# A parameters' stage rearranged: casts and a reciprocal moved between engines, unit 0's table parts sent within SBUF, and a stream loaded later

## The chip, the cores and the metric

The kernel runs on one core of one Trainium2 chip. The metric is the device time of the whole program in microseconds (us), as the median of several runs. Beside the runs there is one profiled execution, in which the hardware profiler records every instruction with its engine, its start and its duration. Engines are named as in the profile: PE (TensorE), DVE (VectorE), ACT (ScalarE), POOL (GpSimd), and SP (SyncE), which only issues DMAs here. "Line L283" is line 283 of the kernel before.

## The reference, cut to what matters

A stream x of 2048 positions by 640 channels passes through four layers: a state-space convolution, a multi-query attention, and both again with the same weights. Each layer normalises its input and adds its result to the stream. What the change touches is the kernel K of the convolution:

```
dt = exp(log_dt)[:, None]                  # 640 channels
logdA = dt * (A_re + 1j * A_im)            # 640 x 128 states
dB = dt * (B_re + 1j * B_im)
P = exp(logdA[:, :, None] * l)             # l = 0 .. 2047
K = einsum("dn,dnl,dn->dl", C, P, dB).real
```

So K[d, l] is a sum over 128 states of |C B dt| exp(dt A_re l) cos(dt A_im l + angle of C B). The rest of a convolution layer is a transform of K and of x, a product, and the transform back, plus x times Dskip.

## The kernel before, in words

**Stages.** `kgen` makes K for all 640 channels and takes about the first 268 us. After it come the first convolution with the spectra of K, an attention layer, the second convolution and the second attention. The change lies in `kgen`, in two places.

**The parameters' stage** (`kg_tables`, L254 to L361). Its tiles are 128 partitions by 640 values: 5 groups of 128 channels, 128 states in each row. It computes five quantities per channel and state: `thr`, the phase step in turns without its whole part; `th1`, the step of 32 positions; `ph`, a phase at the start which contains the angle of C B; `are`, the decay per position; and `lw`, the logarithm of the size of C B dt. The angle comes from an arctangent of the smaller over the larger of |re| and |im|, for which L310 takes a reciprocal on DVE. Each quantity is then split into three BF16 parts whose sum is the float32 value: `cast` writes part k into `hs[n][:, k]` on ACT, `rest` subtracts it on DVE, and so on for three parts. In the kernel before the casts of `ph` and `lw` are `tensor_copy` on DVE.

**The tables.** A unit of work needs the parts with channels in the partitions' place: `tb` (48 rows: three parts of `th1` for 16 channels), `ta` (96 rows: `thr`, then `ph` from row 48) and `tm` (96 rows: `are`, then `lw`). Each is indexed by q, eight groups of 16 partitions of the parameters' tiles. Unit u reads group q = u mod 8. `send` brings `th1`, `thr` and `are` there through DRAM: one DMA writes the whole of `hs[n]` to a DRAM tile `hd...`, and three read it back, one for each part, into all eight q. `send_late` brings `ph` and `lw` straight from SBUF to SBUF, three DMAs of 20 KB for each q. The order on SP in the kernel before: `th1` by DRAM, `thr` by DRAM, the write of `are`, `ph` for q = 0, the three reads of `are`, `lw` for q = 0, and then `ph` and `lw` in turn for q = 1 to 7.

**The units** (`_kgen`, from L394). There are 20 units of 32 channels. For each, PE multiplies the table parts by constants `kg` into PSUM: phases (`phase_first`, L422, one PSUM tile for both halves h) and sizes (`sizes`, L461). DVE turns a phase into an integer fraction of a turn (`turns`, L431, and `fraction`, L436, into tiles `f`), ACT takes sines (`trig`, L446 and L447), squares (L454) and exponentials (`exps`, L469 and L471), DVE multiplies (`products`, L490 to L494), and PE sums over the states (`sums`, L504). `store` (L513) is ACT's copy of a finished unit from PSUM into `kst`; units 0 to 3 share the first `kst`, and `store(0)` stands ahead of all other ACT work in the turn u = 3 of the loop. Sines and exponentials need different activation tables on ACT; each switch is an ACT_TABLE_LOAD. A loop written out by hand (`manual_schedule`) fixes the order of PE, ACT and DVE in the units' loop, and that of ACT, DVE and SP in `kg_tables`. Instructions of the other engines are ordered by the framework, and it is free to place a DMA of SP between those of `kg_tables` where no hand-written order covers it.

**The stream.** `load_x` (L711 to L716) reads x in eight DMAs, two for each group g of four tiles. It is called in the turn u = 0, outside SP's written order, and the framework put its DMAs among those of the parameters' stage: four at the start, one after the write of `th1`, one after that of `thr`, one after `ph` for q = 0, and one after the last `lw`. `stats(t)` are DVE's statistics of tile t of x for the first normalisation: six in the turn u = 0, four in the turn after the last unit, the other six during the first convolution.

**Buffers.** The parameters' tiles live in a pool `kgq` that is closed when `kg_tables` is done; the units' pool `bp` is opened after that and takes the same place in SBUF. The pool's option `reuse_waits="tile"` makes the first writer of each buffer wait for the last users of what lay there. In `kgq` the tiles of `hs` come first, in the order ph, lw, th1, thr, are. In `bp` the two buffers of `kst` come first (8 KB for each partition), then in the kernel before the four of `f` (4 KB each).

Of the kernel before, what the change touches and what calls it, by code (L numbers as in the profile page):

```python
# [21 lines left out]
P = 128  # L22
L = 2048
D = 640
NST = 128
# [177 lines left out]
class Net:  # L203
# [47 lines left out]
        with ExitStack() as ctx:  # L251
            self._kgen(ctx)

    def kg_tables(self, pp, hs, t3, SH, ldt, aim, are_raw, bre, bim, cre, cim, ta, tb, tm):  # L254
# [9 lines left out]
        ar, ai, mx, mn, gt = (t3(n) for n in ("ar", "ai", "mx", "mn", "gt"))  # L264
        res = {n: t3("res" + n) for n in hs}

        def cast(n, src, k):
            A(hs[n][:, k], src if k == 0 else res[n], AF.Copy)

        def rest(n, src, k):  # L270
            V(res[n], src if k == 0 else res[n], hs[n][:, k], ALU.subtract)

        def send(n, dst, between=lambda: None):
            hd = self.dr.tile([P, 3, 5 * NST], BF16, name="hd" + n)
            nc.sync.dma_start(hd, hs[n].rearrange("p k t s -> p k (t s)"))
            between()
            for k in range(3):
                nc.sync.dma_start(dst[16 * k : 16 * k + 16].rearrange("d q t s -> d q (t s)"),
                                  hd[:, k].rearrange("(q d) x -> d q x", d=16))

        def send_late(q, dst, h):
            for k in range(3):
                nc.sync.dma_start(dst[48 + 16 * k : 64 + 16 * k, q].rearrange("d t s -> d (t s)"),  # L283
                                  h[16 * q : 16 * q + 16, k].rearrange("d t s -> d (t s)"))

        A(dt, ldt, AF.Exp)
        for t in range(5):
            T(th[:, t], aim[:, t], dt[:, t : t + 1], 1.0 / TWO_PI, ALU.mult, ALU.mult)
        V(wr, cre, bre, ALU.mult)
        self.frac(pp, thr, th, SH)  # L290
        T(th1, thr, 32.0, None, ALU.mult)
        self.frac(pp, th1, th1, SH)
        cast("th1", th1, 0)
        V(u0, cim, bim, ALU.mult)
        V(wr, wr, u0, ALU.subtract)
        A(ar, wr, AF.Abs)
        V(wi, cre, bim, ALU.mult)
        V(u0, cim, bre, ALU.mult)
        V(wi, wi, u0, ALU.add)
        A(ai, wi, AF.Abs)  # L300
        rest("th1", th1, 0)
        cast("th1", th1, 1)
        V(mx, ar, ai, ALU.max)
        V(mn, ar, ai, ALU.min)
        T(mx, mx, 1e-37, None, ALU.max)
        rest("th1", th1, 1)
        cast("th1", th1, 2)
        send("th1", tb)
        cast("thr", thr, 0)
        nc.vector.reciprocal(u0, mx)  # L310
        V(u0, mn, u0, ALU.mult)
        for t in range(5):
            A(are[:, t], are_raw[:, t], AF.Copy, scale=dt[:, t : t + 1])
        cast("are", are, 0)

        A(u1, u0, AF.Arctan)
        V(gt, ai, ar, ALU.is_gt)
        rest("thr", thr, 0)
        cast("thr", thr, 1)
        T(wr, wr, 0.0, 0.5, ALU.is_lt, ALU.mult)  # L320
        S(u1, gt, 0.5 * math.pi, u1, op0=ALU.mult, op1=ALU.subtract)
        A(u1, u1, AF.Abs, scale=1.0 / TWO_PI)
        T(wi, wi, 0.0, -2.0, ALU.is_lt, ALU.mult)
        rest("thr", thr, 1)
        V(u1, wr, u1, ALU.subtract)
        A(u1, u1, AF.Abs)
        cast("thr", thr, 2)
        send("thr", ta)
        T(ph, th1, 32.0, None, ALU.mult)
        self.frac(pp, ph, ph, SH)  # L330
        S(u1, wi, 1.0, u1, op0=ALU.add, op1=ALU.mult)
        V(ph, ph, u1, ALU.add)
        self.frac(pp, ph, ph, SH)

        A(u2, u0, AF.Square)
        A(lw, mx, AF.Ln)
        A(u3, u2, AF.Ln, bias=1.0)
        nc.vector.tensor_copy(hs["ph"][:, 0], ph)
        rest("ph", ph, 0)
        nc.vector.tensor_copy(hs["ph"][:, 1], res["ph"])  # L340
        rest("ph", ph, 1)
        nc.vector.tensor_copy(hs["ph"][:, 2], res["ph"])
        rest("are", are, 0)
        cast("are", are, 1)
        S(lw, u3, 0.5, lw, op0=ALU.mult, op1=ALU.add)
        for t in range(5):
            T(lw[:, t], lw[:, t], ldt[:, t : t + 1], None, ALU.add)
        rest("are", are, 1)
        cast("are", are, 2)
        send("are", tm, lambda: send_late(0, ta, hs["ph"]))  # L350
        nc.vector.tensor_copy(hs["lw"][:, 0], lw)
        rest("lw", lw, 0)
        nc.vector.tensor_copy(hs["lw"][:, 1], res["lw"])
        rest("lw", lw, 1)
        nc.vector.tensor_copy(hs["lw"][:, 2], res["lw"])
        for q in range(8):
            if q > 0:
                send_late(q, ta, hs["ph"])
            send_late(q, tm, hs["lw"])

    def _kgen(self, ctx):  # L361
        tc, nc, ins = self.tc, self.nc, self.ins
# [8 lines left out]
        kg = sp.tile([96, 2560], BF16, name="kg")  # L371

        with tc.tile_pool(name="kgq", bufs=1) as pp:
            SH = [P, 5, NST]
# [16 lines left out]
            with tc.manual_schedule(engines={mybir.EngineType.Activation, mybir.EngineType.DVE,  # L391
                                             mybir.EngineType.SP}):
                self.kg_tables(pp, hs, t3, SH, ldt, raw["A_A_im"], raw["A_A_re"], bre, bim, cre, cim,
                               ta, tb, tm)  # L394

        bp = ctx.enter_context(tc.tile_pool(name="kgb", bufs=2, reuse_waits="tile"))


        units = [(q, r, q * 256 + 16 * r, 128, 128) for q in range(2) for r in range(8)]
        units += [(2, r, 512 + 16 * r, 64, 64) for r in range(4)]  # L400
        C1, S1, C2, S2, M1, M2, E1R, F, PH, PE_, PK, KST = ({} for _ in range(12))
        KST[0, 0] = bp.tile([P, 64, 32], F32, tag="kst", bufs=2, name="kst00")

        def big(tag, u, x, bufs=2):
# [4 lines left out]

        def fl(a):  # L410
            return a.rearrange("p d a s -> p (d a) s")

        def grp(table, u, par, rows):
            d = units[u][2] + par * units[u][3]
            return table[0:rows, d % 128 // 16, d // 128]

        def phase_first(u, h):

            pp = PH[u, h] = kp.tile([P, 1024], F32, tag="ph", bufs=1, name=f"ph{u}{h}")
            src, col, rows = ((tb, 0, 48), (ta, 512, 96))[h]  # L420
            for par in range(2):
                nc.tensor.matmul(pp[:, 512 * par : 512 * par + 512], grp(src, u, par, rows),  # L422
                                 kg[0:rows, col : col + 512], start=True, stop=True)

        def turns(u, h):

            if (u, h) not in PH:
                phase_first(u, h)
            pp = PH.pop((u, h))
            f = F[u, h] = bp.tile([P, 1024], I32, tag="f", bufs=4, name=f"f{u}{h}")  # L430
            nc.vector.tensor_scalar(f, pp, 2.0**23, None, ALU.mult)  # L431

        def fraction(u, h):

            f = F[u, h]
            nc.vector.tensor_scalar(f, f, 9, 9, ALU.logical_shift_left, ALU.arith_shift_right)  # L436

        def trig(u, h):
            if h == 0:
# [88 lines left out]
        n = len(units)  # L528
        engines = {mybir.EngineType.PE, mybir.EngineType.Activation, mybir.EngineType.DVE}
        with tc.manual_schedule(engines=engines):  # L530
            for h in range(2):
                turns(0, h)
                fraction(0, h)
            left = []

            def fill():
# [3 lines left out]
            for u in range(n + 3):  # L540
                now, nxt, prod, tot = u < n, u + 1 < n, 0 < u <= n, 2 <= u < n + 2
                odd = u % 2 == 1
                if u == 0:
                    self.load_x()
# [163 lines left out]

        return dram.rearrange("(i h t) d -> h i t d", h=2, t=16)

    def load_x(self):  # L711
        nc = self.nc
        for g in range(4):
            for jh in range(2):
                nc.sync.dma_start(self.x[64 * jh : 64 * jh + 64, 4 * g : 4 * g + 4],
                                  self.rows(self.ins["A_u"])[jh][:, 4 * g : 4 * g + 4])  # L716
# [968 lines left out]
```

## Time and profile before

| | us |
|---|---|
| median of 3 runs | 2933.86 |
| lowest and highest | 2932.78, 2934.31 |
| the profiled execution's own time | 2934.5 |
| its span, first to last instruction | 2932.7 |
| busy in the span: PE, ACT, DVE | 2690.0, 2378.7, 2350.0 |
| ACT's first sine (L446) | starts at 46.34 |
| ACT's first write of kst (L513) | starts at 80.34 |
| last write of kst | starts at 268.53 |

How to read the views. The page gives the span and the busy time of each engine. The windows cut the span into stretches: the busy time of each engine with the number of its instructions, the granted clock, the share of the DMA engines that was busy, and GB/s. The timeline lists instructions in order of time: start, duration, engine, line, operation, out<-in by the program's names, and in brackets the idle time of the engine before it with what ended that. An engine's name with a q behind it (SPq, ACTq) stands for its sequencer, which issues DMAs and waits; that is not counted as busy. The waits group idle times: who waited for whom, us in total, times, the longest. For SPq these are the times that the queue of DMA issues stood still. The view of a line gives durations in ns as smallest, median and largest, then the first and last start in us.

### The profile page before, as it was taken

The numbers are of one execution on the slowest core, as the hardware profiler recorded it, in microseconds if no ns is written. First come the engines' busy times: TensorE is split into PE (matmuls) and PEld (weight loads), VectorE is DVE, ScalarE is ACT, GpSimd is POOL, SyncE is SP. The second block draws the span as 40 slices with busy tenths as digits, with TensorE's granted clock in tenths as the row PEclk, the third lists the DMA queues.
The fourth block names the chain that finished last, engine by engine and source line by source line (L and its number), as shares of the span: only waits on it lengthen the run. The fifth ranks groups of instructions, "written<-read, shape, count | busy, mean of one in ns | idle before, by whom it ended". The sixth has DMA issues, their size and how long they took to land. (4 is left out here: it accounts for less than half of the span.)

```text
span 2932.7 us, 71549 instructions
## 1 busy us (share of the span) xinstructions
PE 2690.0 (92%) x29916; PEld 1561.1 (53%) x29916; DVE 2350.0 (80%) x2819; ACT 2378.7 (81%) x2905; POOL 293.9 (10%) x514
## 2 busy tenths in 40 slices
PE   2667989998899999999999998998999999999999
PEld 0335979774344444444444787764444444444444
DVE  8998999935688888878888699726888888888885
ACT  5996432546899999999999624338999999999997
POOL 0000011000111110101011101001101111111111
PEclk9668999998999999999999999998999999999999
DMA  6115544442211111111111346231111111111211
GB/s 148 36 31 159 216 101 108 129 135 71 88 34 34 38 34 34 35 35 33 37 32 31 100 108 164 68 128 47 32 37 38 49 34 35 52 35 36 55 30 32
DMA packets 156101, 196.31 MB, mean 67 GB/s; under 512 B 66220, under 2 KB 123532, under 8 KB 152148
## 3 DMA queue, kind: packets, MB, share of 16 engines
q1 hardware_dynamic: 119704, 141.90, 16.1%
q0 software_dynamic: 33776, 48.08, 7.6%
q8 instruction: 239, 3.92, 0.5%
q10 hardware_dynamic: 2288, 1.64, 0.2%
q14 instruction: 94, 0.77, 0.1%
HBM read 111.47 MB, written 48.55 MB: 55 GB/s over the span
## 5 line engine op out<-in xcount | busy, mean ns | idle before, releaser
L1390 ACT ACTIVATE ring<-ring 128x1024 f32<-128x1024 f32 (+1 forms) x680 | 739.8, 1088 | 0.4 <-DVE ring L1381 0.3
L1365 ACT ACTIVATE pt<-scb 128x1024 f32<-128x1024 f32 x684 | 693.3, 1115 | 25.6 <-PE scb L1355 23.6
L1365 ACT ACTIVATE pt<-scd 128x1024 f32<-128x1024 f32 x684 | 699.9, 1135 | 13.6 <-PE scd L1355 11.8
L1381 DVE COPY ring<-scd 128x1024 f32<-128x1024 f32 x307 | 375.4, 1223 | 81.9 <-PE scd L1355 56.4
L1381 DVE COPY ring<-scb 128x1024 f32<-128x1024 f32 x307 | 374.9, 1221 | 79.8 <-PE scb L1355 59.6
L1355 PE MATMUL scb<-qpb,kt 62*128 62x512 f32 x2048 | 365.3, 445 | 28.8 <-DVE ring L1381 14.1
L1355 PE MATMUL scd<-qpd,kt 62*128 62x512 f32 x2048 | 364.3, 444 | 18.1 <-ACT pt L1365 6.8
L1421 PE MATMUL pob<-pt,vt 128*32 128x256 f32 x5472 | 368.0, 387 | 0.0
L1421 PE MATMUL pod<-pt,vt 128*32 128x256 f32 x5472 | 367.4, 386 | 0.0
L1355 PEld LDWEIGHTS scb<-qpb,kt 62*128 62x128 f32 x2048 | 169.9, 186 | 248.0 <-ACT pt L1365 133.0
L1355 PEld LDWEIGHTS scd<-qpd,kt 62*128 62x128 f32 x2048 | 169.3, 186 | 238.8 <-ACT pt L1365 142.2
L1407 DVE SCALAR_TENSOR_TENSOR zh<-zh,zm 128x1024 f32<-128x1024 f32 x198 | 239.9, 1211 | 0.0
L1421 PEld LDWEIGHTS pob<-pt,vt 128*32 128x32 f32 x5472 | 143.3, 109 | 168.4 <-issue 109.7
L1421 PEld LDWEIGHTS pod<-pt,vt 128*32 128x32 f32 x5472 | 143.2, 109 | 165.9 <-issue 107.1
L1421 PE MATMUL pob<-ring,vt 128*32 128x256 f32 x2456 | 164.8, 381 | 0.4 <-ACT ring L1390 0.4
L1421 PE MATMUL pod<-ring,vt 128*32 128x256 f32 x2456 | 163.9, 379 | 0.4 <-ACT ring L1390 0.4
L1453 POOL DMA_DIRECT2D dn<-on x62 | 43.6, 703 | 1189.0 <-DVE on L1452 1151.8
L1459 POOL DMA_DIRECT2D rc<-ivd x248 | 126.4, 516 | 113.4 <-DMA ivd<-dn 109.4
L1490 DVE TENSOR_TENSOR x<-pyd,x 128x320 f32<-128x320 f32 x147 | 71.8, 488 | 77.2 <-PE pyd L1503 77.1
L1490 DVE TENSOR_TENSOR x<-pyb,x 128x320 f32<-128x320 f32 x147 | 71.8, 489 | 76.5 <-PE pyb L1503 76.4
L1503 PE MATMUL pyb<-wo,ot 128*32 128x320 f32 x1176 | 106.7, 434 | 6.1 <-DVE on L1452 5.5
L1503 PE MATMUL pyd<-wo,ot 128*32 128x320 f32 x1176 | 106.7, 434 | 5.4 <-DVE on L1452 4.6
(388 smaller groups left out, 4086.1 us busy)
## 6 DMA issues: line engine op xcount, KB each, us to landing
Akh<-kh SPq DMA_DIRECT2D x10, 2048.0 KB
rc<-ivd POOLq DMA_DIRECT2D x248, 64.0 KB, 2.2
kh<-Ak SPq DMA_DIRECT2D x5, 2048.0 KB
qhd<-qh SPq DMA_DIRECT2D x40, 256.0 KB
qld<-ql SPq DMA_DIRECT2D x40, 256.0 KB
qpb<-qhd SPq DMA_DIRECT2D x256, 40.0 KB
qpd<-qhd SPq DMA_DIRECT2D x256, 40.0 KB
ot<-on SPq DMA_DIRECT2D x216, 40.0 KB
```

What stands on the lines that cost most here:

```text
L1355: nc.tensor.matmul(sc[:, 512 * par : 512 * par + 512], kt[rows, 128 * t : 128 * t + 128], qps[nb, hg][rows, f].rearrange("p a c -> p (a c) ...
L1365: nc.scalar.activation(pt, sc, AF.Exp, scale=SCALE)
L1381: nc.vector.tensor_copy(cols, sc)
L1390: nc.scalar.activation(cols, cols, AF.Exp, scale=SCALE)
L1407: nc.vector.scalar_tensor_tensor(h, a, c[k], f, op0=ALU.add, op1=ALU.mult)
L1421: nc.tensor.matmul(po[32 * j : 32 * j + 32, 256 * f : 256 * f + 256], v[:, t], pt[j], start=(t == 0), stop=(t == 15))
L1453: nc.gpsimd.dma_start(den, on[20:128:32].rearrange("j (c r) -> j c r", c=32))
L1459: nc.gpsimd.dma_start(inv[32 * j : 32 * j + 32], self.ivd[hg % 2, j : j + 1].to_broadcast([32, 512]))
L1490: nc.vector.tensor_tensor(xh, py, xh, ALU.add)
L1503: nc.tensor.matmul(py[j : j + m], o[:, 128 * i + j : 128 * i + j + m], w[:, c0 : c0 + n], start=start, stop=stop)
```

## The change

- **Reciprocal and angle.** The maximum takes one DVE instruction instead of two. The reciprocal of it is made on ACT as Exp(-Ln(max)), with one correction step on DVE (a multiplication and a combined subtraction and multiplication). Ln of the maximum is so taken early and kept for `lw`.
- **Casts and time steps on ACT.** The three casts of `ph` and of `lw` are done by ACT; so are the scalings by 32 that make `th1` and the start of `ph`, and the addition of log dt to `lw` (five Identity instructions with a bias for each group).
- **Order.** The parts of `are` and `thr` are split earlier, ahead of the end of the angle; `ph` and `lw` are split in turn with each other.
- **SBUF to SBUF for q = 0.** The new `send(q, dst, n, base)` sends three parts of one group. It is used for `th1`, `thr` and `are` with q = 0 as soon as they are split. `put` writes the whole of `hs[n]` to DRAM right behind, and `get` reads groups 1 to 7 back. The nine DMAs of the three gets stand after the last put and ahead of the sends of `ph` and `lw` for q = 0.
- **The stream.** Group 0 of x is loaded at the start; groups 1 to 3 are loaded inside the late stream, two DMAs after each of q = 1, 2 and 3, now in SP's written order. Statistics of tiles 4 and 5 move from the turn u = 0 to the turn u = 19.
- **Unit 0's phases inside `kg_tables`.** `first(h)`, that is `turns` and `fraction` of unit 0, is called between the sends for q = 0 and those for q = 1. The buffers `f` get a pool of their own, `kgf`, ahead of `kgq`; the helper functions move up with them and are otherwise unchanged.

```diff
-        def send(n, dst, between=lambda: None):
-            hd = self.dr.tile([P, 3, 5 * NST], BF16, name="hd" + n)
-            nc.sync.dma_start(hd, hs[n].rearrange("p k t s -> p k (t s)"))
-            between()
+        def send(q, dst, n, base=0):
             for k in range(3):
-                nc.sync.dma_start(dst[16 * k : 16 * k + 16].rearrange("d q t s -> d q (t s)"),
-                                  hd[:, k].rearrange("(q d) x -> d q x", d=16))
-        def send_late(q, dst, h):
...
+                nc.sync.dma_start(dst[base + 16 * k : base + 16 * k + 16, q].rearrange("d t s -> d (t s)"),
+                                  hs[n][16 * q : 16 * q + 16, k].rearrange("d t s -> d (t s)"))
+        def put(n):
+            hd[n] = self.dr.tile([P, 3, 5 * NST], BF16, name="hd" + n)
+            nc.sync.dma_start(hd[n], hs[n].rearrange("p k t s -> p k (t s)"))
+        def get(n, dst):
             for k in range(3):
+                nc.sync.dma_start(dst[16 * k : 16 * k + 16, 1:].rearrange("d q t s -> d q (t s)"),
+                                  hd[n][16:, k].rearrange("(q d) x -> d q x", d=16))
+        self.load_x(range(1))
...
-        V(mx, ar, ai, ALU.max)
-        T(mx, mx, 1e-37, None, ALU.max)
-        nc.vector.reciprocal(u0, mx)
+        S(mx, ar, 1e-37, ai, op0=ALU.max, op1=ALU.max)
+        A(lw, mx, AF.Ln)
+        A(rc, lw, AF.Exp, scale=-1.0)
...
+        V(u0, mx, rc, ALU.mult)
+        V(mn, mn, rc, ALU.mult)
+        S(u0, u0, 2.0, mn, op0=ALU.subtract, op1=ALU.mult)
+        A(u1, u0, AF.Arctan, scale=-1.0)
...
+        send(0, ta, "thr")
+        put("thr")
...
+        send(0, tm, "are")
+        put("are")
+        get("th1", tb)
+        get("thr", ta)
+        get("are", tm)
...
+        for t in range(5):
+            A(u3[:, t], u3[:, t], AF.Identity, scale=0.5, bias=ldt[:, t : t + 1])
+        self.frac(pp, ph, ph, SH)
+        cast("ph", ph, 0)
+        V(lw, u3, lw, ALU.add)
+        rest("ph", ph, 0)
+        cast("lw", lw, 0)
+        cast("ph", ph, 1)
+        rest("lw", lw, 0)
+        rest("ph", ph, 1)
+        cast("lw", lw, 1)
+        cast("ph", ph, 2)
+        send(0, ta, "ph", 48)
         rest("lw", lw, 1)
+        cast("lw", lw, 2)
+        send(0, tm, "lw", 48)
+        for h in range(2):
+            first(h)
+        for q in range(1, 8):
+            send(q, ta, "ph", 48)
+            send(q, tm, "lw", 48)
+            if q < 4:
+                self.load_x(range(q, q + 1))
...
+        fp = ctx.enter_context(tc.tile_pool(name="kgf", bufs=4))
...
                 if u == 0:
-                    for t in range(6):
+                    for t in range(4):
                         self.stats(t)
...
+                if u == n - 1:
+                    for t in range(4, 6):
+                        self.stats(t)
```

More of the change, by code (lines that the diff above doesn't have):

```diff
@@ L288, in kg_tables @@
             T(th[:, t], aim[:, t], dt[:, t : t + 1], 1.0 / TWO_PI, ALU.mult, ALU.mult)
+        self.frac(pp, thr, th, SH)
+        A(th1, thr, AF.Copy, scale=32.0)
         V(wr, cre, bre, ALU.mult)
[L290 to L293, printed above, removed]
         V(u0, cim, bim, ALU.mult)
[L295 to L304, printed above, removed]
-        T(mx, mx, 1e-37, None, ALU.max)
[L306 to L311, printed above, removed]
         for t in range(5):
@@ L314, in kg_tables @@
         cast("are", are, 0)
-        A(u1, u0, AF.Arctan)
+        self.frac(pp, th1, th1, SH)
+        cast("th1", th1, 0)
+        V(wr, wr, u0, ALU.subtract)
+        V(wi, cre, bim, ALU.mult)
+        A(ar, wr, AF.Abs)
+        cast("thr", thr, 0)
+        rest("th1", th1, 0)
+        cast("th1", th1, 1)
+        V(u0, cim, bre, ALU.mult)
+        V(wi, wi, u0, ALU.add)
+        A(ph, th1, AF.Copy, scale=32.0)
+        A(ai, wi, AF.Abs)
+        rest("th1", th1, 1)
+        cast("th1", th1, 2)
@@ L317, in kg_tables @@
+        send(0, tb, "th1")
+        put("th1")
+        S(mx, ar, 1e-37, ai, op0=ALU.max, op1=ALU.max)
+        A(lw, mx, AF.Ln)
+        A(rc, lw, AF.Exp, scale=-1.0)
+        V(mn, ar, ai, ALU.min)
+        rest("thr", thr, 0)
+        rest("are", are, 0)
+        cast("thr", thr, 1)
+        cast("are", are, 1)
+        V(u0, mx, rc, ALU.mult)
+        V(mn, mn, rc, ALU.mult)
+        S(u0, u0, 2.0, mn, op0=ALU.subtract, op1=ALU.mult)
+        A(u1, u0, AF.Arctan, scale=-1.0)
         V(gt, ai, ar, ALU.is_gt)
-        rest("thr", thr, 0)
@@ L329, in kg_tables @@
[L329 to L342, printed above, removed]
@@ new lines, in kg_tables @@
+        T(wi, wi, 0.0, -2.0, ALU.is_lt, ALU.mult)
+        S(u1, wi, 1.0, u1, op0=ALU.add, op1=ALU.mult)
+        self.frac(pp, ph, ph, SH)
+        V(ph, ph, u1, ALU.add)
+        A(u2, u0, AF.Square)
+        A(u3, u2, AF.Ln, bias=1.0)
+        for t in range(5):
+            A(u3[:, t], u3[:, t], AF.Identity, scale=0.5, bias=ldt[:, t : t + 1])
+        self.frac(pp, ph, ph, SH)
+        cast("ph", ph, 0)
[3 more added lines that the diff above has]
+        cast("ph", ph, 1)
@@ L371, in _kgen, with grp, phase_first, turns @@
         kg = sp.tile([96, 2560], BF16, name="kg")
+        fp = ctx.enter_context(tc.tile_pool(name="kgf", bufs=4))
+        units = [(q, r, q * 256 + 16 * r, 128, 128) for q in range(2) for r in range(8)]
+        units += [(2, r, 512 + 16 * r, 64, 64) for r in range(4)]
+        C1, S1, C2, S2, M1, M2, E1R, F, PH, PE_, PK, KST = ({} for _ in range(12))
+        def grp(table, u, par, rows):
+            d = units[u][2] + par * units[u][3]
+            return table[0:rows, d % 128 // 16, d // 128]
+        def phase_first(u, h):
+            pp = PH[u, h] = kp.tile([P, 1024], F32, tag="ph", bufs=1, name=f"ph{u}{h}")
+            src, col, rows = ((tb, 0, 48), (ta, 512, 96))[h]
+            for par in range(2):
+                nc.tensor.matmul(pp[:, 512 * par : 512 * par + 512], grp(src, u, par, rows),
+                                 kg[0:rows, col : col + 512], start=True, stop=True)
+        def turns(u, h):
+            if (u, h) not in PH:
+                phase_first(u, h)
+            pp = PH.pop((u, h))
+            f = F[u, h] = fp.tile([P, 1024], I32, tag="f", bufs=4, name=f"f{u}{h}")
+            nc.vector.tensor_scalar(f, pp, 2.0**23, None, ALU.mult)
+        def fraction(u, h):
+            f = F[u, h]
+            nc.vector.tensor_scalar(f, f, 9, 9, ALU.logical_shift_left, ALU.arith_shift_right)
+        def first(h):
+            turns(0, h)
+            fraction(0, h)
         with tc.tile_pool(name="kgq", bufs=1) as pp:
@@ L393, in _kgen @@
                 self.kg_tables(pp, hs, t3, SH, ldt, raw["A_A_im"], raw["A_A_re"], bre, bim, cre, cim,
-                               ta, tb, tm)
+                               ta, tb, tm, first)
         bp = ctx.enter_context(tc.tile_pool(name="kgb", bufs=2, reuse_waits="tile"))
-        units = [(q, r, q * 256 + 16 * r, 128, 128) for q in range(2) for r in range(8)]
-        units += [(2, r, 512 + 16 * r, 64, 64) for r in range(4)]
-        C1, S1, C2, S2, M1, M2, E1R, F, PH, PE_, PK, KST = ({} for _ in range(12))
         KST[0, 0] = bp.tile([P, 64, 32], F32, tag="kst", bufs=2, name="kst00")
@@ L411, in fl @@
             return a.rearrange("p d a s -> p (d a) s")
[L413 to L436, printed above, removed]
         def trig(u, h):
@@ L709, in rows, with load_x @@
         return dram.rearrange("(i h t) d -> h i t d", h=2, t=16)
-    def load_x(self):
+    def load_x(self, gs):
         nc = self.nc
-        for g in range(4):
+        for g in gs:
             for jh in range(2):
```

31 lines of the change are left out of this document (5 added, 26 removed).

## The prediction

> **What bounds the kernel now.** I read the page first, then the windows of the first stage, its timeline, the waits of the engines and of SP's queue, the line that writes kst, and the end of the stage.
>
> ```profile
> span 2932.7 us, 71549 instructions
> core 0: us, PE busy (x) PEld busy (x) DVE busy (x) ACT busy (x) POOL busy (x), PEclk, DMA share, GB/s
> 0.00:46.00 46.00, 1.40 (x3) 0.33 (x4) 37.29 (x57) 18.89 (x27) 0.73 (x8) 1.00 0.85 198
> 85.00:105.00 20.00, 14.31 (x244) 7.44 (x246) 20.00 (x20) 19.63 (x22) 0.63 (x4) 0.67 0.01 2
> 145.00:165.00 20.00, 12.02 (x275) 6.51 (x275) 19.75 (x20) 19.61 (x21) 0.62 (x4) 0.76 0.30 52
> ```
>
> The profiled run took 2934.5 us, 1.8 more than its span and 0.6 more than the median of 2933.86. The edits lie in the first 80 us and at 255 us. In the first 46 us DVE is busy for 37.29 and ACT for 18.89: DVE sets the parameters' stage. The twenty units after it run at ACT's pace: 19.6 of 20 us busy through the stage. DVE starts with a backlog and has slack by 145. So what ACT gains or loses before its first unit comes out at the end, unless something holds ACT in between.
>
> ```profile
> 5.79 1.07 DVE L288 TENSOR_SCALAR th<-rA_A_im,dt 128x128 f32<-128x128 f32 x5 [5.79 <-DMA rA_A_im<-in_A_A_im]
> 8.25 0.82 DVE L289 TENSOR_TENSOR wr<-rA_C_re,rA_B_re 128x640 f32<-128x640 f32 x1 [1.40 <-DMA rA_B_re<-in_A_B_re]
> 16.99 0.82 DVE L303 TENSOR_TENSOR mx<-ar,ai 128x640 f32<-128x640 f32 x1
> 17.73 0.82 DVE L304 TENSOR_TENSOR mn<-ar,ai 128x640 f32<-128x640 f32 x1
> 19.60 4.15 DVE L310 RECIPROCAL u<-mx 128x640 f32<-128x640 f32 x1
> 31.14 1.28 ACT L336 ACT_TABLE_LOAD   x1
> 36.71 0.49 DVE L342 CAST hph<-resph 128x640 bf16<-128x640 f32 x1
> 40.54 0.74 ACT L268 ACTIVATE hare<-resare 128x640 bf16<-128x640 f32 x1 [1.84 <-DVE resare L271]
> 41.31 0.34 SPq L275 DMA_DIRECT2D hdare<-hare  x1
> 41.74 1.87 SPq L283 DMA_DIRECT2D ta<-hph  x3
> 43.66 0.58 SPq L715 DMA_DIRECT2D x<-in_A_u  x1
> 44.34 1.47 SPq L278 DMA_DIRECT2D tm<-hdare  x3
> 44.36 1.23 DVE L431 TENSOR_SCALAR f<-ph 128x1024 int32<-128x1024 f32 x1 [0.67 <-DMA hdare<-hare]
> 44.90 0.10 PEld L422 LDWEIGHTS <-ta 96*128 96x128 bf16 x1 [13.89 <-DMA ta<-hph]
> 47.94 0.69 DVE L436 TENSOR_SCALAR f<-f 128x1024 int32<-128x1024 int32 x1
> 53.66 1.01 PE L461 MATMUL pe<-kg,tm 48*128 48x512 bf16 x2 [7.02 <-DMA tm<-hdare]
> 54.43 0.21 DVE L725 BATCH_NORM_AGGREGATE mv<-st 128x2 f32<-128x12 f32 x1
> 54.71 1.02 ACT L469 ACTIVATE m<-pe 128x1024 f32<-128x1024 f32 x1 [2.74 <-PE pe L461]
> 55.56 1.23 DVE L431 TENSOR_SCALAR f<-ph 128x1024 int32<-128x1024 f32 x1 [0.92 <-PE ph L422]
> ```
>
> Unit 0's fractions end at 48.63 (47.94 + 0.69). Then ACT loses 2.74 us at L469, because PE waits until 53.66 for parts of tm issued at 44.34 behind a load of x. DVE's six statistics run from there to 54.64, some 1.0 each.
>
> **What hangs on SP.** Three facts of before's trace carry my forecast.
>
> ```profile
> SPq L283 <- DMA x<-in_A_u: 3.0, 1, 3.0
> SPq L275 <- DMA rA_B_re<-in_A_B_re: 1.2, 1, 1.2
> SPq L715 <- DMA rA_C_re<-in_A_C_re: 0.4, 1, 0.4
> 47.69 5.18 SPq L283 DMA_DIRECT2D ta<-hph  x3
> 62.48 1.85 SPq L283 DMA_DIRECT2D ta<-hph  x3
> 71.96 2.72 SPq L283 DMA_DIRECT2D tm<-hlw  x3
> 76.96 1.85 SPq L283 DMA_DIRECT2D tm<-hlw  x3
> L513 ACTq EVENT_SEMAPHORE  x4: 17/38/2439, 77.5 to 80.2; - x4
> 80.34 0.61 ACT L513 ACTIVATE kst<-pk 128x512 f32<-128x512 f32 x1
> POOL c L441 <- ACT are L313: 22.1, 1, 22.1
> ```
>
> First, a DMA waits for the one issued eight places before it to land. Loads of x need nothing of C_re and the write of th1's parts nothing of B_re, yet both waited for them; each stands eight places later in the order of issue. In the same way the send at 47.69 waited 3.0 for the x issued eight places before it, at 43.66.
>
> Second, the last parts of ph and lw leave SP one triple every 1.89 us (0.63 each), and the last of them is issued at 78.22 (76.96 + 2 x 0.63). A send lands 1.9 after its issue starts: the third of 41.74 starts at 43.0, and PE goes on at 44.90. So the last lands at 80.1.
>
> Third, ACT's sequencer waits at L513, the first write of kst, four times from 77.5 to 80.2 and once for 2.44 us, and the write starts at 80.34 directly behind the instruction before it. The unit buffers lie where the parameters' tiles were (POOL's first memset waited 22.1 us for ACT's last use of A_re); kst comes first in its pool and hs["ph"], hs["lw"] first in theirs. The write therefore waits for the late sends to have read them, and in before they end just in time. The change puts its f buffers ahead of both pools alike, so the overlap stays.
>
> **The change, part by part.** *Engines.* DVE loses the reciprocal (4.15), six casts (0.49 each), two scalings by 32 (0.5 each), one maximum (0.5) and the five additions of the time step (1.1), and gains two of 0.82: 8 us less work. ACT takes the casts at 0.74. But now the two alternate. DVE's second product waits for B_im: A_im came at 5.79, B_re at 8.25, so B_im between 9.1, where DVE wants it, and 10.7; I take 10.0. From there nine operations at 0.74 between starts (16.99 to 17.73) and one at 0.5 give the maximum at 17.5. Then ACT: Ln, Exp and a load of tables ahead of each, 2 x (1.28 + 0.74) = 4.0, to 21.5. How many loads there are is not in the trace; from none to two, 0 to 2.6 us. I take two, since each change between Exp, Arctan, Ln and Sin in before has its load. Three dependent DVE operations (2.5), Arctan (0.84), DVE (0.9), Abs (0.8) bring 26.5; the third parts of thr and are follow at 27.7 and 29.1, against 41.28 for are in before. ph needs eight more DVE operations and then three casts and two subtractions in turn with lw's: 37.5, no earlier than the 37.2 of before.
>
> The Trainium skill ("ScalarE: Activation LUTs", the section on table sets) says that one set holds exp and ln both, so Ln then Exp would need one load. By that rule all that follows is 1.3 us earlier and the sum below 1.3 us less; no row of before has the pair.
>
> *SP's queue.* It now holds, in order: three sends of th1, its put, the same for thr and are, nine gets, then three sends of ph and three of lw for unit 0, then the stream for q = 1 to 7 with six loads of x inside. The third part of thr at 27.7 is followed by three sends and a put (2.3), then those of are: the last put goes at 31.9. The nine gets follow all at once, 7/8 of 160 KB each.
>
> ```profile
> ta<-hdthr SPq DMA_DIRECT2D x3, 160.0 KB
> x<-in_A_u SPq DMA_DIRECT2D x4, 640.0 KB
> 12.00:20.00 8.00, 0.00 (x0) 0.00 (x0) 7.86 (x12) 3.23 (x5) 0.00 (x0) 1.00 1.01 224
> 36.00:38.00 2.00, 0.00 (x0) 0.00 (x0) 1.97 (x4) 0.03 (x1) 0.00 (x0) 1.00 1.18 140
> ```
>
> From 36 to 38 only the gets of thr move, at 140 GB/s with the DMA engines full; from 12 to 20 only x, at 224. A get of 143 KB takes 1.04 us, nine 9.4. They start when the last put is written, near 34.3 (hdare's landed within 3.0 of its issue), and end at 43.7. The sends of ph are issued at 37.5 to 39.5, behind them in the queue, and land near 44.5: 0.4 before those of before. With one matmul pair (1.0) and f (1.23 + 0.69) unit 0's fractions end at 47.5, against 48.63.
>
> *Unit 0.* tm's parts are long there, so the 2.74 goes. What is late next is DVE: four statistics (4.0) and then turns(1, 0) at 51.5 instead of 55.56. The head start is 4.0 us, and ACT would want kst at 76.3. The other two statistics, 2.0 us, move to unit 19.
>
> ```profile
> 258.14 2.36 DVE L490 SCALAR_TENSOR_TENSOR e1r<-c,m 128x1024 f32<-128x1024 f32 x2 [2.64 <-ACT c L454]
> ```
>
> There DVE waits 2.64 for ACT: they cost nothing, or up to 2.0 if that idle time is gone.
>
> *The stream.* The eighth get lands at 34.3 + 8 x 1.04 + 1.4 = 44.0 (1.4 from the end of its moving to its landing: an estimate, within the 1.9 that a send takes in all), the ninth at 45.1; by the rule of eight they release the stream's first two sends. The first x follows at 48.3. A load of x moves for 2.9 us (655 KB at 224 GB/s) and lands between 4.8 (2.9 + 1.9) and 7.6 after issue (43.66 to 48.3 + 3.0); I take 6.0, nearer the lower end since no gets run beside it. Two in a row land at 54.3 and 57.2; the second pair, eight places on, must wait for each, though SP would be there at 53.3. So the second pair goes at 54.3 and 57.2 and lands at 60.4 and 63.2; the third goes at 61.6 and 63.2, its second lands at 70.4, and q = 5 waits for that (67.6 without). Sixteen issues of 0.63 later the last goes at 80.5 and lands at 82.4. In before one triple at 71.96 took 0.87 too long, cause not shown: 0 to 0.9; I add 0.4. ACT's sequencer is released at 82.8 instead of 80.1, so kst is written 2.7 us later. ACT stands idle for 6.5 us or so and its head start is gone. The tables themselves come in time: q = 2 lands at 56, unit 2 asks near 60.
>
> **Sum:** 2934.5 + 2.7 = 2937.2 for a profiled run, 2936.6 for the median. Of this, 0.2% or 5.9 us is about what a measurement can tell from no change.
>
> **The rivals.** *The stream does not hold ACT* (shorter landings of x, or kst free earlier): the 4.0 pass through, 2929.9. Against it stands the wait at L513. Chance 0.11.
>
> *Nor do the gets hold unit 0*: the sends of ph land 1.9 after 38.8, the fractions end at 43.8, 7.7 us ahead: 2926.2. Against it, tm's parts at 44.34, which came behind x. Chance 0.09.
>
> *Slower*: x lands 7.6 after issue as the one of 43.66 did. The waits for the second load of each of the three pairs then add 1.6 each, the stream ends 4.8 later, at 87.6: 2941.4. It decides from a last landing at 86. That load had gets behind it, these have only sends. Chance 0.11.
>
> *The gets as fast as x* (0.64 each, 224 GB/s): then not the landing of the gets but the sends of unit 0 hold SP, until 41.3 instead of 44.0; the stream ends 2.7 earlier, ACT is released at 80.1 as in before, and the time is 2933.9. The row of 140 GB/s speaks against it; chance 0.05. The Trainium skill ("DMA: Bandwidth & Descriptors", Specifications) gives 512 B as the least transfer for line rate; the gets' 1,280-byte rows should then run as fast, and the trace disagrees, 140 beside 224.
>
> **The numbers.** My case has 0.64, with 2933 to 2939.5 for its unknown costs: table loads -2.6, B_im -0.9 to +0.7, landing of x -2.8 (no wait at q = 5) to +2, the slow triple +-0.4. The range takes in the first rival below and ends ahead of the slower one: 2929.5 to 2940. Faster by over 0.2%: the second rival alone, 0.09. Slower: 0.11. Within: 0.64 + 0.11 + 0.05 = 0.80.
>
> **What would show it.** Right: in the changed profile ACT's first write of kst has idle time before it of some 6 us, released by a send of hlw, near 83; the 2.74 at L469 is gone; SP's queue shows waits for x between the sends; unit 0's second phase waits for ta behind the gets near 44.5. Wrong: no idle time at kst; sends of ph that land 1.9 after issue; SP's stream over by 76.

## The result and the profile after

| | before | after |
|---|---|---|
| median of 4 runs each, us | 2933.32 | 2959.09 |
| lowest and highest | 2931.89, 2934.31 | 2955.82, 2961.62 |
| profiled execution, own time and span | 2934.5, 2932.7 | 2961.6, 2959.8 |

The ratio is 1.0088, with a 95% interval of 1.0070 to 1.0105. The change costs 25.8 us. The forecast was 2936.6, with a range that ended at 2940.0: the time lies outside it. The main case, with a chance of 0.64, rested on a single wait that makes the kernel 2.7 us slower. One more wait was there, and no term of the prediction stood for it.

First the timeline of the kernel before, at the border between `kgen` and the first convolution. These rows had not been read for the forecast. `kd<-kst` are the stores of the finished kernel K to DRAM, `Rk`, `kts` and `ktl` the pieces of K that POOL's queue loads back for the transform, `zk` the transform's first products, `kh<-Ak` the store of its first result.

```profile
260.24 0.58 POOL L829 DMA_DIRECT2D Rk<-kd  x1 [9.64 <-ACT s L447]
268.48 1.60 PE L667 MATMUL zk<-Rk,wf 128*128 128x128 f32 x12
269.16 12.80 SPq L522 DMA_DIRECT2D kd<-kst  x8
286.49 0.53 POOL L829 DMA_DIRECT2D ktl<-kd  x1 [21.50 <-DMA kd<-kst]
297.24 19.47 SPq L845 DMA_DIRECT2D kh<-Ak  x2
```

Rk is loaded at 260.24, eight microseconds ahead of the last write of kst (268.53), and PE starts on it at 268.48, before the last stores of kst are issued (from 269.16). Now the same places in the timeline of the kernel after, with its first write of kst ahead (line 533 there is L513 before, L848 is L829, L686 is L667).

```profile
81.36 1.85 SPq L276 DMA_DIRECT2D tm<-hlw  x3
84.65 0.60 ACT L533 ACTIVATE kst<-pk 128x512 f32<-128x512 f32 x1 [5.85 <-DMA tm<-hlw]
...
272.69 0.60 ACT L533 ACTIVATE kst<-pk 128x512 f32<-128x512 f32 x1 [6.74 <-PE pk L524]
273.31 7.32 SPq L542 DMA_DIRECT2D kd<-kst  x8
284.10 0.58 POOL L848 DMA_DIRECT2D Rk<-kd  x1 [29.44 <-DMA kd<-kst]
289.13 11.05 PE L686 MATMUL zk<-Rk,wf 128*128 128x128 f32 x71 [16.52 <-DMA Rk<-kd]
320.20 0.34 SPq L864 DMA_DIRECT2D kh<-Ak  x1
```

Two things are to be seen. The first is the one forecast: ACT stands idle for 5.85 us ahead of its first write of kst, released by a send of hlw, and writes at 84.65 instead of 80.34. That is 4.3 us, and it is still there at the last write of kst: 272.69 against 268.53, 4.2 late. The second was not forecast: the load of Rk waits 29.44 us, until the stores of kst have landed, and starts at 284.10 instead of 260.24. PE's first product comes 16.4 us behind the last write of kst (289.13 - 272.69), where in before the two coincided (268.48 and 268.53). So PE starts the convolution 20.65 us late, and the first store of its result goes out 22.96 late (320.20 - 297.24). The two profiled runs differ by 27.1, so 23 of the 27 are there by 320 us. The rest is spread over the later stages and is taken up with the experiments.

**Why Rk waits.** The pool of the units and the pool of the convolution lie in the same stretch of SBUF. By the order and the sizes of the pools, kst lay before at 59,648 to 76,032 (bytes in each partition) and f at 76,032 to 92,416. The convolution puts Rk at 76,032 to 84,224 and kts from there on; what it puts at 59,648 is written late. So in before Rk lay over f, and its wait says so: it was released by ACT's last sine, which reads f. The change opens the pool of f, 16 KB, ahead of the others. Now f lies at 59,648 and kst at 76,032 to 92,416, under Rk and kts. The last unit of K sits in the first buffer of kst, precisely where Rk goes, so Rk can be loaded only when the last unit has been written and stored.

### The profile page after: what moved, and what is told of

Read it like the earlier page. It is cut to its first block, busy times and chain, and to the rows that moved or that the text cites. A ratio compares the mean times of both kernels' runs of the same rounds, so it can differ in the third digit from the quotient of the medians.

```text
span 2959.8 us, 71561 instructions
## 1 busy us (share of the span) xinstructions
PE 2690.6 (91%) x29916; PEld 1562.9 (53%) x29916; DVE 2341.3 (79%) x2806; ACT 2389.3 (81%) x2921; POOL 294.4 (10%) x514
## 5 line engine op out<-in xcount | busy, mean ns | idle before, releaser
L1374 PE MATMUL scb<-qpb,kt 62*128 62x512 f32 x2048 | 365.4, 445 | 30.7 <-DVE ring L1400 13.9
L1472 POOL DMA_DIRECT2D dn<-on x62 | 43.7, 705 | 1192.5 <-DVE on L1471 1155.4
L481 PE MATMUL pe<-kg,tm 48*128 48x512 bf16 (+1 forms) x120 | 54.3, 549 | 63.7 <-ACT m L489 49.1
```

What stands on the lines that cost most here:

```text
L481: nc.tensor.matmul(pe[:, 512 * h : 512 * h + 512], grp(tm, u, par, rows), kg[0:rows, col : col + 512], start=True, stop=True)
L1374: nc.tensor.matmul(sc[:, 512 * par : 512 * par + 512], kt[rows, 128 * t : 128 * t + 128], qps[nb, hg][rows, f].rearrange("p a c -> p (a c) ...
L1472: nc.gpsimd.dma_start(den, on[20:128:32].rearrange("j (c r) -> j c r", c=32))
```

## The experiments

Two theories stood against each other for the 25.8 us. By the first, some 20 us are the layout: the 16 KB of f push kst under Rk. By the second, the convolution only shows what the parameters' stage has lost, and Rk waits because everything ahead of it is late. A second question was where the 4.3 us at kst come from, and a third what the rest of the change is worth without both waits. Seven kernels were run, 5 or 11 times each; the first four below share one series with the kernel before (2932.78, median of 21 runs), the last three another (2932.95, median of 27).

### f on the other side (f_right)

```diff
-        fp = ctx.enter_context(tc.tile_pool(name="kgf", bufs=4))
+        fp = early.enter_context(tc.tile_pool(name="kgf", bufs=4, side="right"))
```

The kernel after, with the buffers of f at the other end of SBUF, so that they push nothing.

> The changed kernel, with the pool of the f buffers on the right side of SBUF instead of ahead of the parameters' tiles. The first kst buffer then lies at 59648 to 67840 again, beneath hs of ph and lw, and Rk of the convolution (76032 to 84224) lies over c1 instead of over kst. Theory A (the place of kst makes Rk's load wait for the last stores of kst): the load of Rk is issued near 265 instead of 284.1, PE's first zk starts near 273 instead of 289.1, 16 to 18.7 us are won; the wait of some 6 us at the first write of kst stays, since kst still lies over hs of ph and lw: 2938 to 2942. Theory B (the place has no part in it: the load waits because the stores of kst end late or the stage runs in another rhythm): no change, 2956 to 2961.

Measured: 2938.70, ratio 1.0020 (1.0011 to 1.0029). From its timeline:

```profile
84.42 0.60 ACT L533 ACTIVATE kst<-pk 128x512 f32<-128x512 f32 x1 [5.73 <-DMA tm<-hlw]
264.99 0.57 POOL L848 DMA_DIRECT2D Rk<-kd  x1 [10.61 <-DMA wf<-in_c_wf]
273.00 14.56 PE L686 MATMUL zk<-Rk,wf 128*128 128x128 f32 x128 [0.84 <-DMA Rk<-kd]
```

The wait of Rk for kst's stores is gone, and with it 20 of the 26 us. The wait at kst is as long as in the kernel after (84.42, idle 5.73), and PE's first product is 4.5 later than in before, as kst is 4.1 later. So the wait of Rk can go while the wait at kst stays, and the layout theory holds.

### Only f moved (f_moved)

```diff
+        fp = ctx.enter_context(tc.tile_pool(name="kgf", bufs=4))
         with tc.tile_pool(name="kgq", bufs=1) as pp:
...
-            f = F[u, h] = bp.tile([P, 1024], I32, tag="f", bufs=4, name=f"f{u}{h}")
+            f = F[u, h] = fp.tile([P, 1024], I32, tag="f", bufs=4, name=f"f{u}{h}")
```

The counterpart: the kernel before with nothing but the pool of f opened first.

> The kernel before, with nothing but the f buffers moved to a pool of their own ahead of the parameters' tiles, as the change does. kst lies at 76032 to 92416, where Rk and the first of kts will lie. Theory A: the load of Rk waits for the last stores of kst, PE's first zk starts at about 285 to 288 instead of 268.5; 16 to 19 us slower, 2949 to 2953. Theory B: within 1 us of the kernel before, 2933.

Measured: 2951.74, ratio 1.0065 (1.0051 to 1.0079), 19.0 us slower than before. Its timeline:

```profile
79.73 0.60 ACT L514 ACTIVATE kst<-pk 128x512 f32<-128x512 f32 x1
268.31 7.27 SPq L523 DMA_DIRECT2D kd<-kst  x8
279.13 0.58 POOL L830 DMA_DIRECT2D Rk<-kd  x1 [28.90 <-DMA kd<-kst]
284.18 16.03 PE L668 MATMUL zk<-Rk,wf 128*128 128x128 f32 x126 [16.56 <-DMA Rk<-kd]
```

Here no instruction is added or moved by hand, `kgen` is as early as before (kst at 79.73), and Rk waits as in the kernel after. So a shift of 16 KB by itself makes 19 us, three quarters of the loss. What is left of the change without this shift was f_right, 5.9 slower than before; the two add up to nearly the whole, 24.9 of 25.8.

### kst ahead of f, the late parts elsewhere (kst_first)

```diff
+        lp = early.enter_context(tc.tile_pool(name="kgl", bufs=1, side="right"))
+        ksp = ctx.enter_context(tc.tile_pool(name="kgk", bufs=2))
         fp = ctx.enter_context(tc.tile_pool(name="kgf", bufs=4))
...
-            hs = {n: pp.tile([P, 3, 5, NST], BF16, name="h" + n)
+            hs = {n: (lp if n in ("ph", "lw") else pp).tile([P, 3, 5, NST], BF16, name="h" + n)
```

The kernel after with kst back in its old place (its tiles come from `ksp`), and with the parts of ph and lw at the other end, so that kst lies over nothing that is sent late. Both waits should go, and what is left is the rest of the change.

> The changed kernel, with kst in a pool of its own ahead of the f buffers (59648 to 76032, f above it), so that both lie where they lay before the change, and hs of ph and lw in a pool on the right side, so that no buffer of the units lies over them. Theory A (two waits, both made by what lies over what): the 5.85 of idle time at the first write of kst and the 16 us more ahead of PE's first zk both go; kst is written near 78.8 instead of 80.3 before the change: 2930 to 2934, the kernel before or 1.5 us better. Theory B (the late stream and the stores are late in themselves): 2950 or more.

Measured: 2932.91, ratio 1.0002 (0.9993 to 1.0011): no difference. Its timeline:

```profile
49.17 1.22 DVE L412 TENSOR_SCALAR f<-ph 128x1024 int32<-128x1024 f32 x1 [6.99 <-PE ph L403]
51.16 1.06 ACT L468 ACTIVATE c<-f 128x1024 f32<-128x1024 int32 x1 [6.72 <-DVE f L417]
79.24 0.61 ACT L535 ACTIVATE kst<-pk 128x512 f32<-128x512 f32 x1
81.33 1.86 SPq L276 DMA_DIRECT2D tm<-hlw  x3
256.23 0.57 POOL L850 DMA_DIRECT2D Rk<-kd  x1 [6.72 <-DVE mv L746]
266.78 1.60 PE L688 MATMUL zk<-Rk,wf 128*128 128x128 f32 x12
```

ACT writes kst at 79.24 without a pause, although the stream's last sends go out only at 81.33: they hold nobody when kst lies elsewhere. That shows that the wait at kst is one for the reading of hs["ph"] and hs["lw"], as the prediction had it. Rk is loaded at 256.23 without waiting for kst's stores. But freed of both waits the change wins 1.1 us at kst and nothing that can be measured at the end. It is held earlier: unit 0's second phase lets DVE wait 6.99 us and ACT 6.72.

### The loads of x behind the stream (x_last)

```diff
-            if q < 4:
-                self.load_x(range(q, q + 1))
+        for q in range(1, 4):
+            self.load_x(range(q, q + 1))
```

The kernel after, with both its layout waits, but the six loads of x after the last send.

> The changed kernel, with groups 1 to 3 of x loaded after the whole late stream (q = 1 to 7) instead of inside it. If the loads of x inside the stream (their issues and the waits of the DMA eight places on) make the last send late, that one lands some 8 to 10 us earlier, near 74 to 76, the 5.85 of idle time at the first write of kst goes, and the kernel takes 2952 to 2955. If the stream is late for another reason (the gets, the sends themselves), the idle time stays and so does the time, 2956 to 2961. The wait of Rk's load stays in both.

Measured: 2950.41, ratio 1.0063 (1.0049 to 1.0077), 8 us better than the kernel after, each against its own runs of before. Its timeline:

```profile
71.70 1.85 SPq L276 DMA_DIRECT2D tm<-hlw  x3
78.47 0.61 ACT L533 ACTIVATE kst<-pk 128x512 f32<-128x512 f32 x1
277.46 0.58 POOL L848 DMA_DIRECT2D Rk<-kd  x1 [28.73 <-DMA kd<-kst]
```

The last sends go out 9.7 us earlier, and kst is written at 78.47 with no pause. So it was the loads of x inside the stream that made its last send, and so kst, late. At kst 6.2 us are won (84.65 - 78.47), more than the 5.85 of the pause. The rest of the 8 came behind `kgen`. The time is 1.6 us below the range that was expected. Rk's wait is untouched.

### The reads moved (kst_first_gets)

```diff
         put("th1")
+        get("th1", tb)
...
         put("are")
-        get("th1", tb)
         get("thr", ta)
-        get("are", tm)
...
         send(0, tm, "lw", 48)
+        get("are", tm)
```

kst_first, with the nine reads from DRAM spread: those of th1 right behind its write, those of are behind unit 0's sends of ph and lw.

> As kst_first, with the gets moved in SP's queue: th1's straight behind its put, thr's behind the put of are, those of are behind the sends of lw for unit 0. Theory: in kst_first ACT stands idle for 6.72 us between its second and third sine, because the sends of ph for unit 0 lie behind nine gets. With three gets ahead of them they land near 42 instead of 48, the idle time shrinks to 1 to 2 us, and unit 0 is 5 to 6 us earlier. Since q = 2 of the stream then follows two loads of x too closely (asked for near 55, landed near 56.5), up to 2 of that are lost: 2927 to 2930. Rival: what comes late for the third sine is not the DMA queue but the splitting of ph (its third part is ready at 40.4 in both), then no more than 1 us is won: 2932 to 2933.

Measured: 2926.99, ratio 0.9981 (0.9972 to 0.9990): 6.0 us faster than before, and the fastest kernel of this study. Its timeline:

```profile
36.84 3.76 SPq L276 DMA_DIRECT2D ta<-hph  x3
44.95 1.06 ACT L468 ACTIVATE c<-f 128x1024 f32<-128x1024 int32 x1 [0.79 <-DVE f L417]
73.03 0.61 ACT L535 ACTIVATE kst<-pk 128x512 f32<-128x512 f32 x1
```

ACT's sines of the second phase start 6.2 us earlier (44.95 against 51.16), with an idle time of 0.79 in place of 6.72, and the 6.2 are still there at kst (73.03 against 79.24). Unit 0's sends of ph have landed when PE starts on them, at 41.89 here and at 48.12 in kst_first, while the third part of ph is ready at nearly the same time (40.1 and 40.4): it was not the splitting. So the reads did hold unit 0, as the prediction's main case said.

### And x behind the stream as well (kst_first_xlast)

The edit of x_last on top of the last kernel.

> As kst_first_gets, and groups 1 to 3 of x after the whole late stream. If the loads of x hold up the stream's tables for units 2 and 3 once unit 0 is early, this wins 1 to 2 us more: 2926 to 2928. If the tables come in time anyway, it is the same as kst_first_gets within 0.5 us.

Measured: 2928.81, ratio 0.9986 (0.9977 to 0.9995); its interval and that of the last kernel overlap. Its timeline:

```profile
69.89 1.85 SPq L276 DMA_DIRECT2D tm<-hlw  x3
72.91 0.60 ACT L535 ACTIVATE kst<-pk 128x512 f32<-128x512 f32 x1
```

The stream ends early, and kst comes within 0.12 us of the kernel without the edit. Where kst does not lie over the parts, a late stream costs nothing: the tables come in time either way. The hoped-for further gain did not come. The median is even 1.8 higher than that of kst_first_gets, where the expectation allowed 0.5; the kernels are equal to 0.13 us up to the first store of the result (see the table below), and why they part behind it was not tried.

### The reciprocal back on DVE (best_recip)

```diff
-        A(lw, mx, AF.Ln)
-        A(rc, lw, AF.Exp, scale=-1.0)
+        nc.vector.reciprocal(rc, mx)
```

kst_first_xlast, with Ln(max) moved to the other Ln.

> As kst_first_xlast, with the reciprocal of the maximum on DVE again (one instruction, some 4.15 us) instead of Exp(-Ln) on ACT, and Ln of the maximum taken beside the second Ln. The trace of the change shows two loads of tables of 1.28 us and two ACTIVATEs of 0.74 from 17.94 to 22.03, so 4.1 us, against 4.15: if the chain through the angle sets unit 0, the time is the same within 0.7 us; DVE's two subtractions that now lie in ACT's time (18.70 to 20.26) would then come ahead of or behind the reciprocal and make the chain up to 1.6 us longer: 2926 to 2930.

Measured: 2931.60, ratio 0.9997 (0.9988 to 1.0006). Its timeline:

```profile
75.47 0.61 ACT L535 ACTIVATE kst<-pk 128x512 f32<-128x512 f32 x1
```

kst comes 2.6 us later than with the reciprocal on ACT (75.47 against 72.91), and the medians differ by 2.8; both are more than the expectation had allowed. Of the 2.6, 0.3 are there before the reciprocal: the maximum starts at 17.14, in kst_first_xlast at 16.81. The other 2.3 lie between the maximum and the first use of its reciprocal, 7.08 us here and 4.83 there. One instruction of 4.15 on DVE takes no longer than the 4.1 of Ln, Exp and their two loads on ACT; but while ACT works, DVE does three other operations (the minimum and two subtractions), which here come behind the reciprocal. The expectation had counted only two of them, 1.6 us. So Exp(-Ln) is a gain of some 2.3 us, once nothing behind it takes the gain away.

### What stays open

The table sets the first store of the convolution's result (`kh<-Ak`), the profiled run's own time and the median, each as a difference from the kernel before (297.24, 2934.5, and the before of the same series).

| kernel | kh<-Ak | profiled run | median |
|---|---|---|---|
| after | +22.96 | +27.1 | +25.8 |
| f_right | +3.96 | +3.7 | +5.9 |
| kst_first | -0.93 | -3.1 | +0.1 |
| f_moved | +16.84 | +13.9 | +19.0 |
| x_last | +15.11 | +12.6 | +17.6 |
| kst_first_gets | -6.83 | -8.4 | -6.0 |
| kst_first_xlast | -6.70 | -6.4 | -4.1 |
| best_recip | -4.47 | -0.3 | -1.4 |

In profiled runs, what comes after the border lies between -3.0 (f_moved: 13.9 - 16.84) and +4.2 (best_recip). In the medians it is always a little against the new kernel, 0.8 to 3.1 us, but this sets a median beside a single profile. Why the later stages take 4.1 longer in the profiled run of the kernel after (27.1 - 22.96) was not settled. Followed through the two profiled runs, the gap grows in steps: 23.2 at the first attention's first score product (711.5 against 688.3), 24.9 at its last (1655.4 against 1630.5), 27.2 at the second attention's last output product (2942.5 against 2915.3). The profiled run was also the slowest of the four of the kernel after, 2.5 above their median. No experiment was made on it.

## Why the prediction was wrong, point by point

**The step that failed** is the sentence "The change puts its f buffers ahead of both pools alike, so the overlap stays". For kst over hs it is true, and f_right against kst_first shows both sides of it. But there is a third pool over the same stretch, that of the convolution, and it did not move along. Against that one the overlap changed, and by f_moved this costs 19.0 us. The step before it had already closed the view: "The edits lie in the first 80 us and at 255 us". The edit of a pool lies wherever its bytes are used again. The trace of before held a hint of this wait: ktl stood 21.50 us behind kd<-kst, free of charge there because it is needed last. None of the rivals held the case. Without this wait, in f_right, the time is 2938.70, 2.1 above the forecast.

**The wait at kst was right in its cause and too small.** Predicted was +2.7 us, measured +4.3. The terms, by these rows of the timeline after (the last one is from before):

```profile
10.53 0.83 DVE L295 TENSOR_TENSOR u<-rA_C_im,rA_B_im 128x640 f32<-128x640 f32 x1 [1.70 <-DMA rA_B_im<-in_A_B_im]
17.94 1.28 ACT L316 ACT_TABLE_LOAD   x1
19.99 1.28 ACT L317 ACT_TABLE_LOAD   x1
21.29 0.74 ACT L317 ACTIVATE rc<-lw 128x640 f32<-128x640 f32 x1
26.04 0.83 DVE L742 BATCH_NORM_STATS2 st<-x 128x6 f32<-128x320 f32 x2
28.98 0.74 ACT L269 ACTIVATE hthr<-resthr 128x640 bf16<-128x640 f32 x1 [0.40 <-DVE resthr L272]
30.45 0.74 ACT L269 ACTIVATE hare<-resare 128x640 bf16<-128x640 f32 x1
36.27 0.16 POOL L461 MEMSET c<- 128x32 f32 x1 [35.82 <-DMA hdare<-hare]
39.62 0.74 ACT L269 ACTIVATE hph<-resph 128x640 bf16<-128x640 f32 x1 [0.15 <-DVE resph L272]
45.98 1.94 SPq L276 DMA_DIRECT2D ta<-hph  x3
47.56 1.01 PE L401 MATMUL ph<-kg,ta 96*128 96x512 bf16 x2 [11.88 <-DMA ta<-hph]
49.86 0.70 DVE L415 TENSOR_SCALAR f<-f 128x1024 int32<-128x1024 int32 x1
50.59 1.06 ACT L466 ACTIVATE c<-f 128x1024 f32<-128x1024 int32 x1 [5.01 <-DVE f L415]
50.93 1.23 DVE L410 TENSOR_SCALAR f<-ph 128x1024 int32<-128x1024 f32 x1 [0.37 <-PE ph L401]
53.91 1.02 ACT L489 ACTIVATE m<-pe 128x1024 f32<-128x1024 f32 x1
48.67 1.06 ACT L446 ACTIVATE c<-f 128x1024 f32<-128x1024 int32 x1 [0.29 <-DVE f L436]
```

| step | predicted | measured |
|---|---|---|
| B_im there | 10.0 | 10.53 |
| Ln and Exp over, with two loads | 21.5 | 22.03 |
| third part of thr, of are | 27.7, 29.1 | 29.72, 31.19 |
| third part of ph | 37.5 | 40.36 |
| sends of ph for unit 0 landed | 44.5 | 47.5 |
| unit 0's fractions over | 47.5 | 50.56 |
| turns(1, 0) | 51.5 | 50.93 |
| stream's first send | 44.0 | 45.98 |
| its last send issued | 80.5 | 82.6 |
| kst written | 82.8 | 84.65 |

- *The two loads of tables* are there, 1.28 us each. The rule of the Trainium skill ("ScalarE: Activation LUTs", the section on table sets) by which one load would do for Ln and Exp is not borne out here; the forecast had taken two from the rows of before.
- *Splitting*: from B_im to the reciprocal the steps come half a microsecond late, those of thr and are 2.0, that of ph 2.9. Four statistics of x stand among DVE's work from 23.53 to 35.59, where the forecast had them after unit 0's fractions. The hand-written order of `kg_tables` does not cover them, and DVE is busy all the time there; that they are the cause of the delay was not tried by itself. They have their good side: turns(1, 0) follows the fractions at once, at 50.93.
- *The reads*: forecast at 34.3 to 43.7. The windows of the kernel after show them from 36 to 46:

```profile
36.00:38.00 2.00, 0.00 (x0) 0.00 (x0) 1.93 (x4) 1.48 (x3) 0.33 (x4) 1.00 1.14 127
38.00:40.00 2.00, 0.00 (x0) 0.00 (x0) 1.94 (x3) 1.84 (x3) 0.00 (x0) 1.00 1.16 106
40.00:42.00 2.00, 0.00 (x0) 0.00 (x0) 1.97 (x3) 1.10 (x2) 0.00 (x0) 1.00 1.17 129
42.00:44.00 2.00, 0.00 (x0) 0.00 (x0) 0.19 (x1) 1.73 (x2) 0.00 (x0) 1.00 1.13 108
45.00:46.00 1.00, 0.00 (x0) 0.00 (x0) 0.00 (x0) 0.58 (x1) 0.00 (x0) 1.00 1.05 110
46.00:47.00 1.00, 0.00 (x0) 0.00 (x0) 0.00 (x0) 0.00 (x0) 0.00 (x0) 1.00 0.19 31
```

  They start 1.7 late, because the write of are lands only at 36.27 (POOL's first memset waits for it), and they move at 106 to 129 GB/s with the DMA engines full, not at 140. So unit 0's sends of ph land at 47.5 and not at 44.5, and this is the term that was mis-sized. Where ACT wanted kst is 84.65 - 5.85 = 78.80, so the head start was 1.5 us and not 4.0. The prediction had read the head start from DVE's turns(1, 0), and those came even earlier than forecast, 4.6 before those of the kernel before (50.93 against 55.56). But ACT could not use it: its sines of unit 0's second phase start at 50.59, 1.9 later than before (48.67), and it reaches the first exponential only 0.8 earlier (53.91 against 54.71). The landing of ph, not turns(1, 0), set ACT's head start; in kst_first_gets, where it comes 6.2 earlier than in kst_first, kst does too.
- *The stream* took as long as forecast: 36.6 us from the first send to the last (45.98 to 82.6), 36.5 in the sum (44.0 to 80.5). The waits for the DMA eight places before are in the waits of SP's queue after, 6.8 us in all, where the sum had 7.1 (1.0, 2.3, 1.0 and 2.8):

```profile
SPq L734 <- DMA x<-in_A_u: 4.8, 3, 2.9
SPq L276 <- DMA x<-in_A_u: 2.0, 1, 2.0
```

  So the release at kst is late by about what the stream's start was late, 2.0, and the sum 2.7 + 2.0 gives the 4.3 within 0.4. The slower rival, with its 4.8 us more of such waits, did not come either.
- *The smaller covers held.* The 2.74 at unit 0's exponential is gone (53.91, no idle time). The two statistics moved to unit 19 cost nothing: DVE had 0.92 us of idle time left behind them.
- *The rivals.* That the gets run as fast as x is refuted by the windows above (by the rule of 512 B in "DMA: Bandwidth & Descriptors" of the Trainium skill their rows of 1,280 bytes should run as fast, and the rows do not agree; but a get also writes only 16 partitions and a load of x 64, so the length of the rows is not the only difference, and no run here parts the two). That the stream does not hold ACT was put at 2929.9; made true in kst_first, it gave 2932.91, since the head start was shorter. That neither stream nor gets hold was put at 2926.2; made true in kst_first_gets it gave 2926.99.

## What to carry to other kernels

A buffer that moves between pools moves every buffer that lies behind it, and each border of stages where those bytes are used again is part of the change: list for every moved buffer who writes that place next and who reads the old contents last. A buffer that is drained last in one stage belongs under what is filled last in the next. In an in-order queue of DMAs, put what the next unit needs ahead of bulk reads, and only then judge the engine work that it was meant to release: the reciprocal on ACT was worth some 2.3 us where neither the reads nor kst held ACT; what it was worth in the change as made was not tried.

## What the runs showed of the hardware that was not expected

- The reads of the tables' parts from DRAM moved at 106 to 129 GB/s in the kernel after, with the DMA engines counted over full (1.05 to 1.17), against 140 in before. There three stood in the queue and here nine, with sends of ph and lw behind them; what makes the difference was not tried.
- A write of 480 KB from SBUF to DRAM took 3.5 us from its issue (32.74) to its landing (36.27).
- Behind the last write of kst, stores, load and first product in series take 16.4 us: the eight stores are issued over 7.3 us and have landed 3.5 after that, and the load of Rk (1 MB) takes 5.0 more until PE starts.
